# Pooled and masked attention feeding a gated layer: one form for every pair of heads, masks loaded apart, weight bits shifted in SBUF, pooled values on two engines, and a new written order

## The chip, the cores and the metric

The kernel runs on one core of a Trainium2 chip. The metric is the time of one execution on the device in microseconds (us), as the median of several runs. A profile is one further execution, recorded by the hardware profiler; its span is the time from the first to the last instruction.

## The reference

```python
def attention(q, k, v):              # 8 batches, 8 heads, 576 positions, 64 numbers per head
    q_d, k_d, v_d = means of four neighbouring positions           # 144 positions
    out_d = softmax(q_d @ k_d.T / 8) @ v_d
    scores = where(abs(i - j) < 4, q @ k.T / 8, -1e9)              # a band of seven keys
    return repeat(out_d, 4) + softmax(scores) @ v

def gated(x):                        # x: 8 x 576 x 512, the heads side by side
    h = gelu(x @ w_in)               # w_in 512 x 1024
    u, v = halves of h
    v = (v - mean(v)) / sqrt(var(v) + 1e-6) * g_ln
    v = w_sg @ v + b_sg              # w_sg 576 x 576, over positions
    return x + (u * v) @ w_out       # w_out 512 x 512
```

`w_in` and `w_out` reach the kernel as 64-bit floats, seen as pairs of 32-bit words; all else is fp32.

## The kernel before, in words

**Attention.** The eight heads of a batch go in pairs: four pairs per batch, 32 pairs in all, numbered g = 0 to 31. The local part takes a pair in ten tiles of 58 queries by 64 keys. Each pair runs through short tasks, named by letters and the pair's number:

- `lq`, `lk`, `lv`, `lw` load q, k and two layouts of v. `qs` and `ks` sum q and k over four positions (line 391 on VectorE, lines 394 and 395 on Pool). `vs` pools v in four additions (lines 408 and 409, Pool).
- `S` are the local scores (line 424), `Y` the pooled scores (line 445), both on TensorE; `YS` is one task with both.
- `ma` and `mb` add the mask to the scores and move them from PSUM to SBUF (line 432, VectorE). `mx` and `my` take the maxima (lines 454 to 456, 466 and 468, VectorE), `nx` and `ny` turn them into biases, `ea`, `eb` and `ec` are the exponentials (lines 484 and 492, ScalarE), `re` and `rc` the sum and its reciprocal (lines 497 to 503), `np` and `nq` divide.
- `T`, `U`, `t` transpose the probabilities on TensorE (lines 512 and 521); `pa`, `pb`, `pc`, `pe` copy them out (line 221). `D` multiplies them by the values (line 573 the pooled part, line 589 the local part, TensorE). `oe`, `od`, `xa`, `xb` put both parts together into x (lines 554 to 596), and `xh`, `xl`, `xc` split x into a high and a low part for products of three terms (lines 221 and 608).

**Early forms.** `EARLY_S` and `EARLY_D` are 4: pairs 0 to 3 differ from the others. Their mask is put into PSUM by TensorE, as a product of an identity matrix with the mask (line 417), and the scores are added on top of it. Their maxima (`mx`) are read from PSUM, and so are their exponentials. Their v is not pooled: line 573 runs once for each of the four positions of a group, so `D` has four times as many pooled products, with `v4` in place of `vd`; and `lv` loads v in four transfers, not two.

**Weights.** Twelve blocks of the 64-bit weights (`y0` to `y3`, `z0` to `z3`, `r0` to `r3`) are turned into fp32: `w` loads, `wq` scales the high word (line 305 on VectorE, line 303 on ScalarE), `wu` treats the low word, `wb` shifts the bits in two VectorE operations (line 309 writes a PSUM buffer, line 311 reads it and the word and writes SBUF), `wt` adds both (Pool, line 319), `wh` and `wl` split the result into a high and a low part.

**The gated layer** of batch b follows its four pairs: `v` (line 691, the products in batch 0 in four pieces `vk`), its gelu, its statistics (lines 721 to 760; line 740 normalises on VectorE), `u`, `s` and `o` (line 769) with their own tasks, and the stores `os`. Its first product, v of batch b, needs the low part of x of the batch's last pair, so `xl3` for batch 0 and `xl7` for batch 1.

**What sets the order.** `ORDER` is a string that names every task once, with an engine where a task has a choice (`/V` VectorE, `/P` Pool, `/A` ScalarE, `/S` SP). Tasks are issued in its order; each engine works through its own in that order. `place` walks the same string and gives each task its buffers out of 8 of PSUM (`ps`), 10 (`X`) and 38 (`R`) of SBUF. `T` is TensorE. SP issues nearly all loads. One constant, `small`, holds the masks, the identity, two turning matrices and g, and is one transfer.

## Time and profile before

| | before |
|---|---|
| median of 3 runs | 589.13 us |
| runs, from and to | 587.82 to 589.57 us |
| span of the profiled execution | 585.7 us |
| TensorE busy | 559.7 us (96% of the span) |
| VectorE busy | 432.7 us (74%) |
| ScalarE busy | 354.0 us (60%) |
| Pool busy | 306.2 us (52%) |

The span leaves out what lies around the program: it is 3.4 us below the median of the runs. In rows of the profile PE is TensorE, PEld its loading of weights, DVE is VectorE, ACT ScalarE, POOL GpSimd (here Pool) and SP the engine that issues loads. L573 is line 573. A group of instructions reads: line, engine, operation, output and input by the program's names, tile, shape, type, count, then busy time, mean ns of one, and the engine's idle time just before them with what ended it. A row of waits reads: engine, tile and line that waited, what released it, and the total, the number and the longest of these waits.

### The profile page before, as it was taken

The page shows a single profiled execution, that of the slowest core. Times are in us where ns is not written, and L with a number is a line of the kernel's source. Part 1 is how long each engine was busy: PE and PEld are TensorE (multiplying, and loading weights), DVE is VectorE, ACT ScalarE, POOL GpSimd, SP SyncE. Part 2 cuts the span into 40 slices and gives each one's busy share as a digit, 9 for nine tenths or more (in the row PEclk, how much of TensorE's full clock was granted, in tenths as well). Part 3 has the DMA queues.
Part 4 walks back from the last instruction along what each step waited for, and adds up shares of the span by engine and source line. Part 5 has one row for each costly group of instructions (what it writes and reads, how often), then busy time and mean ns, then how long its engine had stood idle before and what let it go on. Part 6 is the DMA issues. An engine that isn't in the chain of part 4 may idle for free.

```text
span 585.7 us, 17441 instructions
## 1 busy us (share of the span) xinstructions
PE 559.7 (96%) x6992; PEld 522.2 (89%) x6992; DVE 432.7 (74%) x947; ACT 354.0 (60%) x1227; POOL 306.2 (52%) x384
## 2 busy tenths in 40 slices
PE   4778999999999999999999999999999999999997
...
DVE  3957998968795998886658786777668877652662
...
PEclk9879999999999999999999999999999999999999
DMA  8999014534503321242046052241117430300103
GB/s 318 305 281 286 14 48 128 158 118 137 144 26 98 97 83 58 96 157 63 16 134 193 13 194 90 59 134 42 37 62 230 118 100 1 113 1 1 41 2 121
DMA packets 30610, 63.21 MB, mean 108 GB/s; under 512 B 3520, under 2 KB 3776, under 8 KB 30528
## 3 DMA queue, kind: packets, MB, share of 16 engines
...
q10 hardware_dynamic: 576, 1.23, 0.6%
q14 instruction: 27, 0.22, 0.1%
...
## 4 chain that ended last, share of the span: by engine, by line
PE 81%; DVE 8%; ACT 5%; issue 3%; DMA 1%; POOL 0%; SPq 0%; ACTq 0%; DVEq 0%; POOLq 0%
PE ps L769 49%; PE ps L691 15%; PE ps L573 4%; ACT X L484 3%; PE ps L512 3%; PE ps L589 3%; PE ps L424 2%; PE ps L445 2%; PE ps L521 2%; DMA small_sb<-in_small_dram 1%; ACT pd L492 1%; DVE R L740 1%; DVE wsg_l L352 1%; DVE st L721 1%; ACT L492 1%
## 5 line engine op out<-in xcount | busy, mean ns | idle before, releaser
L769 PE MATMUL ps<-wsg_h,R 128*128 128x288 f32 x576 | 120.8, 297 | 0.0
L769 PE MATMUL ps<-R,weight_r 128*128 128x288 f32 x768 | 109.4, 297 | 0.3 <-ACT pd L492 0.3
L769 PE MATMUL ps<-X,weight_z 128*128 128x288 f32 x512 | 108.2, 296 | 0.3 <-DVE X L432 0.3
L769 PEld LDWEIGHTS ps<-R,weight_r 128*128 128x128 f32 x768 | 103.8, 188 | 2.1 <-DVE R L826 0.4
L691 PE MATMUL ps<-weight_y,X 128*128 128x512 f32 x320 | 98.0, 400 | 0.1
L484 ACT ACTIVATE X<-X,nb 128x64 f32<-128x64 f32 x280 | 93.5, 338 | 3.2 <-DVE nb L463 2.8
L769 PEld LDWEIGHTS ps<-wsg_h,R 128*128 128x128 f32 x576 | 94.2, 188 | 0.2
L769 PE MATMUL ps<-wsg_l,R 128*128 128x288 f32 x320 | 92.8, 296 | 0.4 <-DVE wsg_l L352 0.4
L769 PEld LDWEIGHTS ps<-X,weight_z 128*128 128x128 f32 x512 | 83.9, 188 | 1.2 <-ACT weight_z L221 0.7
L769 PE MATMUL ps<-R,weight_z 128*128 128x288 f32 x256 | 75.4, 295 | 0.0
L691 PEld LDWEIGHTS ps<-weight_y,X 128*128 128x128 f32 x320 | 58.2, 189 | 12.5 <-POOL X L221 0.4
L769 PEld LDWEIGHTS ps<-wsg_l,R 128*128 128x128 f32 x320 | 60.2, 188 | 0.6 <-DVE wsg_l L352 0.6
L732 POOL TENSOR_TENSOR rs<-rs,nhalf 128x1 f32<-128x1 f32 (+1 forms) x40 | 24.5, 614 | 63.0 <-DVE rs L723 62.9
L807 DVE SCALAR_TENSOR_TENSOR vs<-ps,small_sb,b_sb 128x288 f32<-128x288 f32 x64 | 32.4, 513 | 32.6 <-PE ps L769 31.6
L484 ACT ACTIVATION_READ_ACCUMULATOR X<-X,nb 128x1 f32 x280 | 53.1, 190 | 0.0
L691 PE MATMUL ps<-weight_y,R 128*128 128x512 f32 x128 | 50.7, 396 | 0.0
L408 POOL TENSOR_TENSOR pairs<-R 112x256 f32<-112x256 f32 x56 | 44.6, 796 | 10.2 <-DMA R<-in_v_dram 10.2
L788 ACT ACTIVATE R<-ps 128x288 f32<-128x288 f32 x64 | 24.7, 411 | 40.9 <-PE ps L769 40.8
L221 ACT CAST R<-R 128x512 fp32r<-128x512 f32 (+2 forms) x44 | 28.0, 641 | 34.0 <-DVE R L814 14.2
L769 PEld LDWEIGHTS ps<-R,weight_z 128*128 128x128 f32 x256 | 48.1, 188 | 0.3
L826 POOL TENSOR_TENSOR R<-R,R 128x576 fp32r<-128x576 f32 x21 | 31.1, 1484 | 28.6 <-PE ps L521 14.4
L814 POOL TENSOR_TENSOR R<-R,vs 128x288 f32<-128x288 f32 x23 | 20.4, 894 | 45.2 <-DVE vs L807 39.2
...
## 6 DMA issues: line engine op xcount, KB each, us to landing
...
```

What stands on the lines that cost most here:

```text
L221: (nc.scalar.copy if e == "A" else ENG[e].tensor_copy)(**kw)
L408: ENG[e].tensor_tensor(out=pairs, in0=v[:, 0:2], in1=v[:, 2:4], op=ALU.add)
L484: nc.scalar.activation(out=st["ms"][:, t, :], in_=src, func=AF.Exp, bias=st["nb"][:, t:t + 1], scale=scale, accum_out=sums[par][:, t:t + 1])
L512: nc.tensor.matmul(out=out, lhsT=st["ms"][0:LD, 2 * c:2 * c + 2, :], rhs=turn_l, is_transpose=True, start=True, stop=True)
L573: nc.tensor.matmul(out=out, lhsT=lhsT, rhs=pdt[ks, probs, h * QC:(h + 1) * QC], start=first, stop=last)
L691: nc.tensor.matmul(out=acc, lhsT=r32(l), rhs=r32(weights[f"y{k}"][:, 0, w]), start=(i == 0 and ks[0] == 0), stop=(i == len(ops) - 1 and ks ...
L732: nc.gpsimd.tensor_tensor(out=rs[0:n], in0=rs[0:n], in1=nhalf[0:n], op=ALU.pow)
L769: nc.tensor.matmul(out=acc[:, 0:HALF], lhsT=r32(l), rhs=r32(r), start=(first and n == 0), stop=(last and n == len(ops) - 1))
L788: nc.scalar.activation(out=us[i // 2][:, half(i)], in_=at["ps", "m", b, "u", i][:, 0:HALF], func=AF.Gelu_apprx_tanh)
L807: nc.vector.scalar_tensor_tensor(out=vsb[i], in0=at["ps", "m", b, "s", i][:, 0:HALF], scalar=g_sb[:, i // 2:i // 2 + 1], in1=b_sb[:, half( ...
L814: ENG[e].tensor_tensor(out=u[:, half(i)], in0=u[:, half(i)], in1=vsb[i], op=ALU.mult)
L826: ENG[e].tensor_tensor(out=r32(gl[d]), in0=us[d], in1=gh[d], op=ALU.subtract)
```

## The change

- `EARLY_S`, `EARLY_D` and all that depends on them are gone. Every pair runs `YS`, adds its mask on VectorE (`ma`, `mb`), takes maxima and exponentials from SBUF, and pools its v.
- `small` is split: the masks are a constant of their own, `mask`, in its own transfer; the identity is gone; `small` keeps the turning matrices and g. Both may be loaded from SP or ScalarE.
- The shift of the weight bits (`wb`) writes the SBUF buffer of the result and works in it; the PSUM buffer is gone.
- `vs` may run on VectorE or Pool. The new string gives pairs 0, 1, 2, 5 and 6 to VectorE, 3, 4 and 7 to Pool; of all 32 pairs, 16 go to each.
- The loads of the first four pairs may be issued by ScalarE's queue; before, those of the first two.
- The string `ORDER` is new throughout.

```diff
-wy0 lk0/A lq0/A lq1/A small ks0/P wqy0/A wuy0 wby0 wty0 wy3 qs0/V S0 mx0 lw1/A qs1/P nx0/V ea0 why0/V wqy3/V Y0 my0
...
-EARLY_S, EARLY_D = 4, 4
...
-    small_sb = const.tile([P, 7 * KB + P + LD + 2 * QD + KT], F32, name="small_sb")
...
+    mask_sb = const.tile([P, 7, KB], F32, name="mask_sb")
+    small_sb = const.tile([P, LD + 2 * QD + KT], F32, name="small_sb")
...
-    add("small", {"S": 0.5}, lambda e: nc.sync.dma_start(out=small_sb, in_=small), mb=0.4)
+    add("mask", {"S": 0.5, "A": 0.5}, lambda e: DQ[e].dma_start(out=mask_sb.rearrange("p t k -> p (t k)"), in_=masks), mb=0.22)
+    add("small", {"S": 0.5, "A": 0.5}, lambda e: DQ[e].dma_start(out=small_sb, in_=small), mb=0.17)
...
-        keys = ("R", "w", t), ("ps", "b", t)
+        key = "R", "w", t
...
         def shift(e):
-            bits, done, hw = like(buf(*keys[1])).bitcast(I32), like(buf(*keys[0])).bitcast(I32), word(1)
-            nc.vector.tensor_scalar(out=bits, in0=hw.bitcast(I32), scalar1=3,
+            done, hw = like(buf(*key)).bitcast(I32), word(1)
+            nc.vector.tensor_scalar(out=done, in0=hw.bitcast(I32), scalar1=3,
                                     scalar2=0x7FFFFFF8, op0=ALU.logical_shift_left, op1=ALU.bitwise_and)
-            nc.vector.scalar_tensor_tensor(out=done, in0=hw.bitcast(I32), scalar=-0x80000000, in1=bits,
+            nc.vector.scalar_tensor_tensor(out=done, in0=hw.bitcast(I32), scalar=-0x80000000, in1=done,
                                            op0=ALU.bitwise_and, op1=ALU.bitwise_or)
...
-                for rows in (slice(0, QC), slice(HD, QD)) if early_d else (slice(0, QD),):
-                    DQ[e].dma_start(out=st["v4"][i][rows], in_=v4[b, p, i, rows].rearrange("j (f d) -> j f d", f=FAC))
+                DQ[e].dma_start(out=st["v4"][i], in_=v4[b, p, i].rearrange("j (f d) -> j f d", f=FAC))
...
-            if early:
-                for i in range(2):
-                    nc.tensor.matmul(out=sp[i][:, 0:NW[i] * KB], lhsT=ident_sb, rhs=mask_sb[:, MB[i]:MB[i] + NW[i], :],
-                                     start=True, stop=False, skip_group_check=True)
-            for t in (0, 4, 1, 5, 2, 6, 3, 7, 8, 9) if early else (4, 5, 0, 6, 1, 7, 2, 8, 3, 9):
+            for t in (4, 5, 0, 6, 1, 7, 2, 8, 3, 9):
...
-            if early:
-                for i in range(2):
-                    nc.vector.tensor_reduce(out=stats[par][:, i * NA:i * NA + NW[i]], in_=spv(i), axis=AX.X, op=ALU.max)
-            else:
-                nc.vector.tensor_reduce(out=stats[par][:, 0:NT], in_=st["ms"], axis=AX.X, op=ALU.max)
+            nc.vector.tensor_reduce(out=stats[par][:, 0:NT], in_=st["ms"], axis=AX.X, op=ALU.max)
...
-                    src = spv(i)[:, c] if early else st["ms"][:, t, :]
-                    nc.scalar.activation(out=st["ms"][:, t, :], in_=src, func=AF.Exp, bias=st["nb"][:, t:t + 1],
+                    nc.scalar.activation(out=st["ms"][:, t, :], in_=st["ms"][:, t, :], func=AF.Exp, bias=st["nb"][:, t:t + 1],
...
-                lhsT = st["v4"][t][ks, f, hs] if early_d else st["vd"][ks, t, hs]
...
-            for f in fs:
-                for i in range(2):
-                    for h in range(2):
-                        pooled(i, h, f, 0, slice(0, 3), slice(0, 3))
+            for i in range(2):
+                for h in range(2):
+                    pooled(i, h, 0, slice(0, 3), slice(0, 3))
...
-        if not early_d:
-            add(N("vs"), {"P": 2.7}, vsum, [N("lv"), N("D", 2)], gives=[("R", "v4", g, 0), ("R", "v4", g, 1)])
+        add(N("vs"), {"P": 2.7, "V": 1.1}, vsum, [N("lv"), N("D", 2)], gives=[("R", "v4", g, 0), ("R", "v4", g, 1)])
```

The start of VectorE's queue, before: `nb0` and `stats0` belong to pair 0's local softmax, `weight_y0` is the first weight block, `qd0` holds the row sums of q.

```order
L309 TENSOR_SCALAR ps0_127<-weight_y0_113 128x512
L311 SCALAR_TENSOR_TENSOR R3_128<-weight_y0_113,ps0_127 128x512
L391 TENSOR_REDUCE qd0_75<-R1_117 128x144
L454 TENSOR_REDUCE stats0_79<-ps1_135 128x4
L454 TENSOR_REDUCE stats0_79<-ps2_136 128x6
L463 TENSOR_SCALAR nb0_90<-stats0_79 128x10
```

And after; the lines of the changed code stand a few above those of before (L387 sums, L423 adds the mask, L443 and L453 to L455 take maxima, L305 to L311 are the weights).

```order
L387 TENSOR_REDUCE qd0_76<-R0_114 128x144
L387 TENSOR_REDUCE qd1_77<-R2_119 128x144
L453 TENSOR_REDUCE stats0_80<-ps2_128 128x2
L455 TENSOR_REDUCE stats0_80<-ps3_129 128x1
L462 TENSOR_SCALAR nbd0_93<-stats0_80 128x3
L423 TENSOR_TENSOR X0_206<-ps0_138,mask_sb_70 128x256
L423 TENSOR_TENSOR X0_206<-ps1_139,mask_sb_70 128x384
L443 TENSOR_REDUCE stats0_80<-X0_206 128x10
L305 TENSOR_SCALAR weight_y2_210<-weight_y2_210 128x512
```

The row sums of two pairs and the whole first softmax now stand ahead of the first weight block, and the masks are added here.

The first product D (pair 0) in TensorE's queue, before: R15 and R16 hold the unpooled values, R17 the transposed pooled probabilities. Each of these rows stands four times in a turn; two of the first kind, and one of each other, are shown.

```order
L573 MATMUL ps7_413<-R17_386,R15_377 64x144 x2
L573 MATMUL ps5_414<-R17_386,R15_377 64x144 x2
L573 MATMUL ps7_413<-R17_386,R15_377 64x144 x2
L573 MATMUL ps5_414<-R17_386,R15_377 64x144 x2
...
L573 MATMUL ps7_413<-R17_386,R16_378 64x48 x2
L573 MATMUL ps5_414<-R17_386,R16_378 64x96 x2
...
L589 MATMUL ps7_413<-R14_364,X3_383 64x58 x2
```

And after, where L555 is the pooled part, L570 the local one, and vd0 holds the pooled values of pair 0.

```order
L555 MATMUL ps1_467<-R17_423,vd0_86 64x144 x2
L555 MATMUL ps3_468<-R17_423,vd0_86 64x144 x2
L555 MATMUL ps1_467<-R17_423,vd0_86 64x48 x2
L555 MATMUL ps3_468<-R17_423,vd0_86 64x96 x2
L570 MATMUL ps1_467<-R10_357,X4_464 64x58 x2
```

32 pooled products have become 8, and `vd0` has to be there first.

Between the third products of batch 0 and batch 1's first in TensorE's queue, after (L742 are the products `u`, `s` and `o`, here `s` with wsg_h and wsg_l; L436 and L416 are scores, L664 is v): the first row ends `s` of one half, and the last begins batch 1.

```order
L742 MATMUL ps7_1753<-wsg_l_74,R30_1290 128x288
L555 MATMUL ps3_1778<-R36_1773,vd1_87 64x144 x2
...
L570 MATMUL ps1_1779<-R16_1740,X9_1424 64x58 x2
L742 MATMUL ps5_1808<-wsg_h_73,R28_1129 128x288
...
L742 MATMUL ps5_1808<-wsg_l_74,R30_1290 128x288
L436 MATMUL ps4_1845<-kd0_84,qd0_76 64x144 x2
...
L416 MATMUL ps6_1856<-R17_1513,R25_1420 64x64 x2
L664 MATMUL ps1_1889<-weight_y0_380,X1_1731 128x512 x2
```

In before the third products of batch 0 end at a row of wsg_l as well, and what follows them is this, up to a product `o` of batch 0 and then batch 1.

```order
L769 MATMUL ps5_1581<-wsg_l_73,R18_1376 128x288
L512 MATMUL ps4_1597<-small_sb_70,X8_1191 128x122 x4
L573 MATMUL ps6_1602<-R13_1470,vd1_86 64x144 x2
...
L445 MATMUL ps7_1632<-kd1_84,qd1_76 64x144 x2
...
L769 MATMUL ps0_1946<-R1_1698,weight_r2_1540 128x288
...
L691 MATMUL ps7_2081<-weight_y0_172,X5_1378 128x512 x2
```

Most of batch 0's `o` products stand ahead of batch 1's v before, and all of them behind it after.

More of the change, by code (lines that the diff above doesn't have):

```diff
@@ L189 @@
[L189 to L192 removed]
+lq0/S lk0/A qs0/V lq1/A qs1/V lk1/S mask/S ks0/P YS0 my0 ny0/V ks1/P YS1 ec0 lq2/S qs2/P ma0 mb0 mx0 wy2 wqy2/V wuy2
@@ new lines @@
+ny9/V lw11 s0.5 mx8 xh6/A xl6/P pc7/A pe7/A qs11/V mb9 D7 s0.6 ec9 wqr2/A oe7/A od7 xa7 xb7 nx8/A ea8 gh0.1/A xh7/V
+sa0.5 gh0.0/A wur1 YS10 ma10 whr3/A eb8 xl7/V v1.0 v1.2 sm0.5/V sa0.7 re8/A ks11/P wbr0 u1.4 mx9 nx9/V ea9 wbr2 v1.1
+my10 ny10/V wbr1 wtr1 xc6 lk12 rc8 mb10 eb9 ks12/V ua1.4 vg1.2 vg1.0 nq8/V wtr0 np8/P sm0.4/P xc4 vg1.1 wur2 whr1/A
+u1.6 T8 ua1.6 mx10 xc7 sm0.7/P vb1.0 U8 vb1.1 u1.7 t8 nx10/A ea10 sa0.6 u1.5 vs8/P re9/V pa8/V pb8/V pc8/A pe8/A vs9/V
+wlr3/V ec10 xc5 eb10 gl0.0/P rc9 nq9/P ua1.5 v1.4 va1.4/V wtr2 whr2/A YS11 my11 gh0.2/V ny11/A vb1.2 ma11 vj1.4
@@ L212 @@
     w_out: bass.AP,
+    masks: bass.AP,
     small: bass.AP,
@@ L330, in weight64 @@
         add(f"wq{t}", {"A": 0.56, "V": 0.7}, scaled, [f"w{t}"])
-        add(f"wb{t}", {"V": 1.42}, shift, [f"wq{t}"], takes=keys, gives=keys[1:])
+        add(f"wb{t}", {"V": 1.42}, shift, [f"wq{t}"], takes=[key])
         add(f"wt{t}", {"P": 1.3}, total, [f"wb{t}", f"wu{t}"])
         add(f"wh{t}", {"A": 0.56, "V": 0.4}, high, [f"wt{t}"])
-        add(f"wl{t}", {"P": 1.3, "V": 0.66}, low, [f"wh{t}"], gives=keys[:1])
+        add(f"wl{t}", {"P": 1.3, "V": 0.66}, low, [f"wh{t}"], gives=[key])
     for k in range(KT):
@@ L363, in attention @@
         g = b * NPAIR + p
-        N = lambda c, back=0: f"{c}{g - back}" if g >= back and not (c == "vs" and g - back < EARLY_D) else None
+        N = lambda c, back=0: f"{c}{g - back}" if g >= back else None
         par = g % 2
-        SN = lambda back=0: N("S" if g - back < EARLY_S else "YS", back)
-        YN = lambda back=0: N("Y" if g - back < EARLY_S else "YS", back)
-        early, early_d = g < EARLY_S, g < EARLY_D
         def load_q(e):
@@ L424, in scores @@
                     nc.tensor.matmul(out=sp[i][os, c * KB:(c + 1) * KB], lhsT=q[hs, t * QB:t * QB + KB],
-                                     rhs=k[hs, t * QB:t * QB + KB], start=not early, stop=True,
-                                     skip_group_check=early)
+                                     rhs=k[hs, t * QB:t * QB + KB], start=True, stop=True)
         def masked(i):
@@ L638, in attention @@
-        add(N("mx"), {"V": 0.95 if early else 0.8}, top, ([SN()] if early else [N("ma"), N("mb")]) + [N("nx", 2)])
+        dq = {"S": 0.5, "A": 0.5} if g < 4 else {"S": 0.5}
+        add(N("lq"), dq, load_q, [N("YS", ahead), N("qs", ahead)], takes=[("R", "q", g)], mb=0.3)
+        add(N("lk"), dq, load_k, [N("YS", ahead), N("ks", ahead)], takes=[("R", "k", g)], mb=0.3)
+        add(N("lv"), dq, load_v4, [N("D", ahead // 2)], takes=[("R", "v4", g, 0), ("R", "v4", g, 1)], mb=0.3)
+        add(N("lw"), dq, load_vw, [N("D", ahead)], takes=[("X", "vw", g)], mb=0.33)
```

281 lines of the change are left out of this document (131 added, 150 removed).

## The prediction, made before the changed kernel ran

> **What bounds the kernel now.** I read the page's first two parts, then the windows, then the waits of the first 60 us, then the order of both programs. The page first: its row of engines, and TensorE, VectorE, clock and DMA in 40 slices of 14.6 us each.
>
> ```profile
> PE 559.7 (96%) x6992; PEld 522.2 (89%) x6992; DVE 432.7 (74%) x947; ACT 354.0 (60%) x1227; POOL 306.2 (52%) x384
> ...
> PE   4778999999999999999999999999999999999997
> ...
> DVE  3957998968795998886658786777668877652662
> ...
> PEclk9879999999999999999999999999999999999999
> DMA  8999014534503321242046052241117430300103
> ```
>
> TensorE is full from slice 5 on and not before; the loads fill slices 1 to 4. The windows: each stretch and its length, the busy time (and instructions) of TensorE, its weight loads, VectorE, ScalarE and Pool, the granted clock, the DMA share and GB/s:
>
> ```profile
> 60.00:100.00 40.00, 39.31 (x363) 36.52 (x363) 37.57 (x71) 36.95 (x101) 29.48 (x32) 1.00 0.20 60
> 5.00:100.00 95.00, 81.02 (x1192) 70.17 (x1193) 76.38 (x159) 74.89 (x277) 67.71 (x74) 0.93 0.63 202
> 100.00:200.00 100.00, 98.67 (x1437) 91.70 (x1436) 81.51 (x186) 75.00 (x281) 62.00 (x80) 1.00 0.37 113
> 0.00:100.00 100.00, 81.02 (x1192) 70.17 (x1193) 76.77 (x162) 76.17 (x278) 68.87 (x82) 0.93 0.63 200
> ...
> 60.00:500.00 440.00, 436.20 (x5494) 409.98 (x5494) 349.39 (x771) 302.40 (x1023) 237.54 (x301) 1.00 0.31 95
> ```
>
> Of 26.0 us in which TensorE does nothing (585.7 less 559.7), 19.0 lie in the first 100 us, and only 3.8 between 60 and 500 us. So two things count: how much TensorE has to do, and when it can go on without a gap. From 60 to 100 us VectorE is busy for 37.57 of 40 us and TensorE for 39.31: both are at their end there. Who waits for what before 60 us, TensorE first, then VectorE:
>
> ```profile
> PE ps L417 <- DMA small_sb<-in_small_dram: 8.5, 1, 8.5
> PE ps L573 <- issue: 5.2, 2, 3.1
> ```
>
> ```profile
> DVE ps L309 <- ACT weight_y L303: 5.5, 1, 5.5
> DVE da L556 <- PE ps L589: 5.1, 3, 2.7
> DVE R L221 <- PE ps L521: 4.3, 2, 4.1
> DVE stats L454 <- PE ps L424: 2.5, 1, 2.5
> ```
>
> VectorE stands still for 17.4 us in these four rows, 11.9 of them for TensorE, whose early products (L417, L573) are the ones that the change takes away.
>
> **The change, part by part.** *TensorE loses work.* The forms that go and the one that stays, whole run:
>
> ```profile
> L573 PE MATMUL ps<-R,vd 48*64 48x144 f32 x224 | 13.7, 305 | 0.0
> ...
> L573 PE MATMUL ps<-R,vd 48*64 48x96 f32 x112 | 9.3, 243 | 0.0
> L573 PE MATMUL ps<-R,vd 48*64 48x48 f32 x112 | 7.6, 211 | 0.0
> L573 PE MATMUL ps<-R,R 48*64 48x144 f32 x128 | 7.1, 340 | 2.4 <-issue 2.0 <-DVE X L432 0.3
> L573 PE MATMUL ps<-R,R 48*64 48x96 f32 x64 | 4.5, 289 | 0.0
> L417 PE MATMUL ps<-small_sb 128*128 128x384 f32 x8 | 4.1, 602 | 0.3 <-DVE R L311 0.3
> L573 PE MATMUL ps<-R,R 48*64 48x48 f32 x64 | 3.4, 248 | 3.1 <-issue 3.1
> L417 PE MATMUL ps<-small_sb 128*128 128x256 f32 x8 | 3.3, 502 | 8.5 <-DMA small_sb<-in_small_dram 8.5
> ```
>
> Mask products 4.1 + 3.3, unpooled values 7.1 + 4.5 + 3.4: 22.4 us go. The pooled form costs (13.7 + 9.3 + 7.6) / 28 = 1.09 us per pair, 4.4 us for four pairs. Net 18.0 us less. If every idle gap stayed, the span would be 567.7 us.
>
> *The gaps will not stay.* All 18 us lie before 60 us, where TensorE waits anyway. What counts is when batch 1's first product (v1.0) can begin; behind it TensorE has work without a gap in either order. In the old order, batch 0's third products (s0) end at 101.61 us. The new order has more ahead of v1.0: scores of four more pairs (YS7 to YS10), D of pairs 5 to 7, and the turns T, U, t of pairs 6 and 7. Their lengths, at full clock, from the timeline of before, where one stands behind the other: T from 101.61, D from 102.12, YS from 103.11, U from 104.29 to 104.67, t from 106.34 to 106.46:
>
> ```profile
> 101.61 0.58 PE L512 MATMUL ps<-small_sb,X 122*128 122x122 f32 x4
> 102.12 0.63 PE L573 MATMUL ps<-R,vd 48*64 48x144 f32 x15
> ...
> 103.11 0.29 PE L445 MATMUL ps<-kd,qd 64*64 64x144 f32 x1
> ...
> 104.29 0.32 PE L512 MATMUL ps<-small_sb,X 122*128 122x122 f32 x1
> ...
> 104.67 1.83 PE L769 MATMUL ps<-R,weight_r 128*128 128x288 f32 x12
> 106.34 0.35 PE L521 MATMUL ps<-small_sb,pd 112*112 112x112 f32 x2
> 106.46 1.84 PE L769 MATMUL ps<-R,weight_r 128*128 128x288 f32 x12
> ```
>
> T is 0.51, D 0.99, YS 1.18, U 0.38, t 0.12. Four YS, three D and two of each turn are 4.72 + 2.97 + 2.02 = 9.7 us; at the 98.67% of the 100 to 200 us window, 9.8. So before has done the same work at 111.4 us, and 474.3 us follow.
>
> *VectorE sets the new place.* v1.0 needs the low half of x of pair 7 (xl7, on VectorE). By the order, 209 VectorE instructions stand from the first row sum to xl7. Before's VectorE took 76.77 us for 162 in its first 100 us (474 ns each) and 81.51 for 186 in the next (438 ns). Taken together, 455 ns: 95.1 us of work, bounds 91.6 and 99.1. That count holds what the change adds on VectorE: masks added and a maximum of SBUF in place of two maxima of PSUM in four pairs, and four pooling additions in each of pairs 0, 1, 2, 5 and 6. When can it start? The first transfer of k and its row sum on Pool, before:
>
> ```profile
> 6.19 0.67 POOL L394 TENSOR_TENSOR half<-R 128x288 f32<-128x288 f32 x1 [4.50 <-DMA R<-in_kT_dram]
> 6.93 0.43 POOL L395 TENSOR_TENSOR kd<-half 128x144 f32<-128x144 f32 x1
> ```
>
> q of pair 0 should land about then too, as the first on SP. VectorE makes two row sums, then waits for YS0, which cannot start before kd is there (7.4) and takes 1.18: about 1 us is lost. Counted as one late start: between 5.4 (less load ahead of it) and 7.1 us; I take 6.6. How dense is VectorE behind it? 37.57 / 40 = 0.94 where it is the one at its end (60 to 100 us), 76.38 / 95 = 0.80 over 5 to 100 us, with the 11.9 us of waits for TensorE in it. TensorE is no longer short of time in the new order: it has 81.0 - 18.0 + 9.8 = 73 us to do by v1.0. So I take 0.94: 95.1 / 0.94 = 101.2, v1.0 at 107.8 us instead of 111.4. Span 107.8 + 474.3 = 582.1; with the 3.4 us between the profiled span (585.7) and the median (589.13), **585.5 us, 0.6% faster**. Of 18 us taken away, 14 go into waiting.
>
> *The shift of the weight bits.* Nine of its twelve stand ahead of v1.0. What runs there, and the nearest forms with both sides in SBUF:
>
> ```profile
> L740 DVE TENSOR_SCALAR R<-R,mv,rs 128x512 f32<-128x512 f32 x32 | 20.8, 654 | 2.8 <-POOL rs L732 2.7
> ...
> L309 DVE TENSOR_SCALAR ps<-weight_z 128x512 int32<-128x512 int32 x4 | 2.8, 689 | 0.3 <-ACT pd L492 0.3
> ...
> L305 DVE TENSOR_SCALAR weight_z<-weight_z 128x512 f32<-128x512 f32 x1 | 0.4, 361 | 0.0
> ```
>
> From 689 ns the first operation goes to 361 at best (L305), and by L740's mean, of the same shape in a busy stretch, to 654. I take the second, 0.3 us in all; the first would give 3.0. Both stay in the range. The Trainium skill (VectorE: DVE Perf Modes, "The perf-mode tier table") says that a one-input fp32 operation on VectorE runs at twice the rate when both sides are in SBUF, and not with PSUM on one side. By that alone the place would come 3.0 us earlier; L305's row agrees with it, L740's mean of the same shape does not.
>
> *Company on SBUF.* The same operation on 13 columns, VectorE, twice:
>
> ```profile
> 39.62 0.16 DVE L499 TENSOR_SCALAR sums<-sums 128x13 f32<-128x13 f32 x1
> ...
> 93.50 0.85 DVE L499 TENSOR_SCALAR sums<-sums 128x13 f32<-128x13 f32 x1
> ```
>
> The second is 0.69 us longer. The change puts 20 pooling additions and nine two-input shifts of SBUF on VectorE ahead of v1.0, while Pool runs. If a quarter of the 29 lose 0.69 us each it is 5.0 us, which would end the gain; the mean of 455 ns holds such losses at before's rate, so I add nothing and keep 5 us for the upper end. The Trainium skill (GPSIMD Engine Reference, "Specifications") says that Pool shares its SBUF interfaces with VectorE and contends with VectorE instructions of two SBUF inputs or in a two-port mode; that rule speaks against this change, and the 0.85 us row bears it out.
>
> *Transfers, ScalarE, tail.* By the sizes of the loads that stand ahead of v1.0 in the new order, about 23 MB come in by then; the values of the first four pairs come in two transfers each, not four, so SP issues eight fewer. Pool pools v of three of the first eight pairs, where it did four. At before's pace, 17.60 MB in 62 us (row below), that is 81 us: hidden by 27 us of VectorE's time. ScalarE's exponentials of four pairs read SBUF in place of PSUM; it has the same work as before otherwise and is hidden by VectorE; if it were not, it would cost its own delay one to one. In the last batch nothing of the change applies; I leave before's idle time there, with 2 us to either side for the new order.
>
> ```profile
> DMA packets 8330, 17.60 MB, mean 284 GB/s; under 512 B 960, under 2 KB 960, under 8 KB 8320
> ```
>
> **The rivals.** *A, the whole 18 us come through* (571.1 us): TensorE's gaps stay as they are. For it: 5.2 us of TensorE's early waits sit inside the very products that go, and they leave more room. Against: 209 VectorE instructions would have to be done by 93 us, at a density of 1.10. Only cheaper instructions would allow it. Chance 0.12.
>
> *B, VectorE falls behind and the kernel gets slower.* The place is VectorE's queue in the first 100 us. It works in order, and between its own steps it waits for exponentials of ScalarE, products at a low clock (PEclk begins 9, 8, 7, 9) and Pool. The point from which it decides: 95.1 / (111.4 - 6.6) = 0.907 of density. Below that the new order loses. At before's own 0.80 it is v1.0 at 125.5, span 599.8, 603.2 us; at 0.87, 593.7. For it: 0.80 is what VectorE reached in before. Against: 11.9 us of its waits were for TensorE; with them taken out of the 95 us it is 76.38 / 83.1 = 0.92. Chance 0.26.
>
> *C, the loads set the pace as they do now* (589 us, no change): if SP's queue, where a load that waits for a free buffer holds back those behind it, loses the 27 us. For it: the DMA row is full in slices 1 to 4. Against: it is not in slices 5 and 6. Chance 0.12.
>
> **How the numbers follow.** The forecast has 0.50. About 0.3% (1.8 us) is what a measurement can tell from no change. Of the forecast's 0.50, 0.42 is faster by more than that and 0.08 within; A adds 0.12 faster; B 0.21 slower and 0.05 within; C 0.10 within and 0.02 slower. Faster 0.54, within 0.23, slower 0.23. The range reaches from 576 (v1.0 at 98: the 91.6 us of work, and the shifts at their best) to 597 (a density of 0.84), and leaves out about half of A and the slow end of B.
>
> **What would show it.** Right: TensorE's busy time is near 542 us and its idle time near 40; v1.0's first product (weight_y, 128x512, after a row of wsg products) starts near 108 us; VectorE is at 0.94 from 10 to 105 us; the waits for L417 and "issue" at L573 are gone. Wrong: v1.0 before 102 us or after 113; VectorE waiting for ScalarE or DMA for over 10 us in the first 100; the shift's first operation at 0.4 us throughout; more than 12 us of idle TensorE time behind v1.0.

## The result and the profile after

The changed kernel takes 608.81 us (median of 4 runs, 607.55 to 609.30) beside 588.48 us for the kernel before (now the median of 4 runs): ratio 1.0351, interval 1.0319 to 1.0383. It is 3.5% slower; forecast were 585.5 us and a range of 576 to 597. The lines of the changed code are new: L742 are the products u, s and o, L664 is v, L436 and L416 are scores, L555 and L570 are D, L423 adds the mask, L462 is the pooled bias, L404 and L405 pool v, L589 is the low half of x.

The page after: engines, and TensorE, VectorE, clock and DMA in 40 slices of 15.2 us.

```profile
span 607.5 us, 17056 instructions
...
PE 565.5 (93%) x6784; PEld 522.6 (86%) x6784; DVE 466.4 (77%) x999; ACT 348.5 (57%) x1218; POOL 307.4 (51%) x367
...
PE   3679989699999999999999999999999998999997
...
DVE  5999999989988775895688789686747757683652
...
PEclk9659999899999999999999999999999998999999
DMA  8997356001282223320142414530045222000302
```

VectorE is at 9 in each of slices 2 to 8, where before had 9, 5, 7, 9, 9, 8 and 9; TensorE has a hole in slice 8. Batch 1's first product, which was forecast at 107.8 us, comes at 119.4. The windows ahead of it and behind it (columns as before):

```profile
20.00:120.00 100.00, 81.58 (x1181) 69.51 (x1180) 96.12 (x181) 72.49 (x278) 74.39 (x78) 0.86 0.64 188
0.00:119.40 119.40, 90.34 (x1408) 77.48 (x1408) 109.20 (x211) 82.77 (x328) 86.23 (x101) 0.86 0.69 209
119.40:607.50 488.10, 475.17 (x5378) 445.11 (x5376) 357.25 (x789) 265.77 (x891) 221.22 (x266) 0.99 0.25 79
```

VectorE is as dense as was assumed (96.12 of 100 us; 0.94 in the forecast), and the number of its instructions is right (211; 209 counted from the first row sum). But each takes 109.20 / 211 = 518 ns of busy time, not 455. Behind the place 488.1 us follow, 13.8 more than the 474.3 of the forecast. The two misses, 11.6 and 13.8 us, are the whole error of the span (607.5 less 582.1).

What VectorE waits for up to 130 us, and TensorE's largest waits there:

```profile
DVE qd L387 <- DMA R<-in_qT_dram: 5.1, 2, 4.1
DVE X L423 <- PE ps L416: 1.3, 2, 0.7
```

```profile
PE ps L436 <- POOL kd L391: 8.0, 2, 6.7
PE ps L496 <- POOL X L490: 4.0, 1, 4.0
PE ps L555 <- DVE vd L405: 3.7, 5, 1.5
PE ps L436 <- ACT pd L476: 3.3, 1, 3.3
```

The waits of VectorE that the prediction quoted (17.4 us) are gone, TensorE's for L417 and for "issue" at L573 as well. Behind its first loads VectorE hardly waits any more; its instructions got longer. The groups of the added work up to 119.4 us, and the row sums (L387) for comparison:

```profile
L404 DVE TENSOR_TENSOR pairs<-R 112x256 f32<-112x256 f32 x10 | 8.6, 856 | 0.0
...
L462 DVE TENSOR_SCALAR nbd<-stats 128x3 f32<-128x3 f32 x4 | 6.9, 1731 | 0.0
...
L405 DVE TENSOR_TENSOR vd<-pairs 112x128 f32<-112x128 f32 x10 | 5.7, 574 | 0.3
...
L311 DVE SCALAR_TENSOR_TENSOR R<-weight_z,R 128x512 int32<-128x512 int32 x4 | 4.5, 1117 | 0.1
L311 DVE SCALAR_TENSOR_TENSOR R<-weight_y,R 128x512 int32<-128x512 int32 x4 | 3.9, 980 | 0.1
...
L309 DVE TENSOR_SCALAR R<-weight_y 128x512 int32<-128x512 int32 x4 | 3.1, 764 | 0.0
...
L387 DVE TENSOR_REDUCE qd<-R 128x144 f32<-128x576 f32 x4 | 3.0, 745 | 5.1 <-DMA R<-in_qT_dram 5.1
```

L404 takes 362 ns at its fastest and 856 on average; the two-input half of the shift 691 and 1117. A bias of three numbers takes 1731 on average, because one took 6.40 us. It stands beside Pool like this; VectorE first, then Pool:

```profile
107.43 0.46 DVE L787 TENSOR_TENSOR R<-R,vs 128x288 f32<-128x288 f32 x1
107.81 6.40 DVE L462 TENSOR_SCALAR nbd<-stats 128x3 f32<-128x3 f32 x1
114.13 0.80 DVE L443 TENSOR_REDUCE stats<-X 128x10 f32<-128x640 f32 x1
```

```profile
107.65 0.56 POOL L405 TENSOR_TENSOR vd<-pairs 112x128 f32<-112x128 f32 x1
108.17 2.79 POOL L589 TENSOR_TENSOR R<-R,X 128x576 fp32r<-128x576 f32 x2
110.92 1.29 POOL L319 TENSOR_TENSOR R<-R,weight_r 128x512 int32<-128x512 int32 x1
112.17 1.40 POOL L589 TENSOR_TENSOR R<-R,X 128x576 fp32r<-128x576 f32 x1
113.52 0.66 POOL L390 TENSOR_TENSOR half<-R 128x288 f32<-128x288 f32 x1
114.27 0.42 POOL L391 TENSOR_TENSOR kd<-half 128x144 f32<-128x144 f32 x1
```

Pool's five instructions from 108.17 to 114.19 start without a pause; the first pause is at 114.19 to 114.27, ahead of L391, which needs the result of the instruction in front of it. There the bias ends. ScalarE's exponentials wait for it, and TensorE's scores for them:

```profile
114.31 0.38 ACT L476 ACTIVATE pd<-ps,nbd 128x144 f32<-128x144 f32 x1 [6.30 <-DVE nbd L462]
```

```profile
115.56 0.46 PE L436 MATMUL ps<-kd,qd 64*64 64x144 f32 x4 [3.27 <-ACT pd L476]
```

Take each of VectorE's instructions up to the place, and its duration less the shortest of its own line, names and shape in the run. The sum is 31.3 us, against 8.7 in before up to 111 us. Without it the 211 instructions would average (122.2 - 31.3) / 211 = 431 ns and before's 184 would average (96.8 - 8.7) / 184 = 479 ns (their durations overlap a little at the ends), so the new mix is not longer by itself. 27.6 of the 31.3 us lie on arithmetic instructions from SBUF to SBUF with one or two inputs; no instruction with PSUM on a side and no reduction took over 0.08 us more than its shortest.

The 6.40 us are the exception among these delays. 23 instructions ahead of the place took 0.4 us or more over their shortest; for 21 of them the delay ends with the one Pool instruction that ran when they began (0.08 to 0.17 us ahead of its end). In 12 of the 23 the next Pool instruction follows without a pause, as here (VectorE, then Pool):

```profile
102.11 1.63 DVE L311 SCALAR_TENSOR_TENSOR R<-weight_r,R 128x512 int32<-128x512 int32 x1
```

```profile
101.93 1.26 POOL L490 TENSOR_TENSOR X<-X,rc 128x640 f32<-128x640 f32 x1 [2.52 <-ACT nbd L460]
103.14 1.36 POOL L493 TENSOR_TENSOR pd<-pd,rc 128x432 f32<-128x432 f32 x1
```

At its shortest this L311 takes 0.69 us, so it got in at about 103.0, and it is the Pool instruction behind it that took 0.45 us over its shortest. In before, 6 instructions up to 111 us were so late.

**Theory 1:** VectorE's instructions with two SBUF inputs, and its short one-input ones from SBUF to SBUF, stand behind Pool's; the change put many of them beside a busy Pool. Some of the expectations below say it more strictly, that they start only when Pool pauses; the 12 above contradict that. **Theory 2:** VectorE has too much to do by then, whatever Pool does. **Theory R and F,** on the part behind: the new order of the rest is slower by itself (R), or the late front carries on (F).

### The profile page after: what moved, and what is told of

Read it like the earlier page. It is cut to its first block, busy times and chain, and to the rows that moved or that the text cites. A ratio compares the mean times of both kernels' runs of the same rounds, so it can differ in the third digit from the quotient of the medians.

```text
span 607.5 us, 17056 instructions
## 1 busy us (share of the span) xinstructions
PE 565.5 (93%) x6784; PEld 522.6 (86%) x6784; DVE 466.4 (77%) x999; ACT 348.5 (57%) x1218; POOL 307.4 (51%) x367
## 3 DMA queue, kind: packets, MB, share of 16 engines
q1 hardware_dynamic: 30384, 61.69, 32.7%
## 4 chain that ended last, share of the span: by engine, by line
PE 39%; DVE 5%; ACT 4%; POOL 1%; issue 1%; DMA 0%; ACTq 0%; POOLq 0%
PE ps L742 27%; PE ps L664 6%; ACT X L468 2%; PE ps L570 1%; PE ps L496 1%; PE ps L555 1%; POOL R L733 1%; PE ps L436 1%; PE ps L505 1%; DVE vd L405 1%; PE ps L416 1%; ACT R L222 1%; DMA R<-in_kT_dram 0%; ACT L761 0%; DVE R L816 0%
## 5 line engine op out<-in xcount | busy, mean ns | idle before, releaser
L742 PE MATMUL ps<-wsg_h,R 128*128 128x288 f32 x576 | 123.8, 301 | 3.2 <-DVE R L577 1.5
L742 PE MATMUL ps<-X,weight_z 128*128 128x288 f32 x512 | 112.7, 301 | 3.8 <-DVE X L423 2.4
L468 ACT ACTIVATE X<-X,nb 128x64 f32<-128x64 f32 x320 | 107.0, 340 | 10.2 <-DVE nb L450 9.8
L742 PE MATMUL ps<-R,weight_r 128*128 128x288 f32 x768 | 108.8, 297 | 0.7 <-DVE R L799 0.7
L742 PEld LDWEIGHTS ps<-R,weight_r 128*128 128x128 f32 x768 | 103.4, 188 | 2.3 <-DVE R L799 1.1
L664 PE MATMUL ps<-weight_y,X 128*128 128x512 f32 x320 | 98.9, 404 | 1.2 <-DVE R L577 0.5
L742 PEld LDWEIGHTS ps<-wsg_h,R 128*128 128x128 f32 x576 | 93.9, 188 | 5.2 <-DVE R L577 1.7
L742 PE MATMUL ps<-wsg_l,R 128*128 128x288 f32 x320 | 92.7, 295 | 0.4 <-POOL wsg_l L352 0.4
L742 PEld LDWEIGHTS ps<-X,weight_z 128*128 128x128 f32 x512 | 85.6, 190 | 5.6 <-DVE X L423 2.7
L742 PE MATMUL ps<-R,weight_z 128*128 128x288 f32 x256 | 76.0, 297 | 0.0
L664 PEld LDWEIGHTS ps<-weight_y,X 128*128 128x128 f32 x320 | 58.9, 191 | 14.0 <-DVE weight_y L326 0.9
L468 ACT ACTIVATION_READ_ACCUMULATOR X<-X,nb 128x1 f32 x320 | 61.4, 192 | 0.0
L742 PEld LDWEIGHTS ps<-wsg_l,R 128*128 128x128 f32 x320 | 60.3, 188 | 0.6 <-POOL wsg_l L352 0.6
L222 ACT CAST R<-R 128x512 fp32r<-128x512 f32 (+2 forms) x44 | 27.5, 639 | 53.1 <-POOL R L787 27.6
L664 PE MATMUL ps<-weight_y,R 128*128 128x512 f32 x128 | 51.4, 401 | 0.4 <-DVE R L589 0.4
L742 PEld LDWEIGHTS ps<-R,weight_z 128*128 128x128 f32 x256 | 48.7, 190 | 0.6
L490 POOL TENSOR_TENSOR X<-X,rc 128x640 f32<-128x640 f32 x25 | 33.8, 1351 | 27.6 <-DVE rc L487 17.4
L222 ACT COPY R<-ps 112x192 f32<-112x192 f32 (+3 forms) x71 | 26.1, 391 | 32.1 <-PE ps L505 15.5
L436 PE MATMUL ps<-kd,qd 64*64 64x144 f32 (+2 forms) x512 | 28.9, 294 | 16.7 <-POOL kd L391 8.0
```

The costliest lines, as they stand in the source:

```text
L222: (nc.scalar.copy if e == "A" else ENG[e].tensor_copy)(**kw)
L436: nc.tensor.matmul(out=st["sdv"][n][os, cs], lhsT=qd2[par][hs, i * QC:i * QC + HD], rhs=st["kd"][hs, ks], start=True, stop=True)
L468: nc.scalar.activation(out=st["ms"][:, t, :], in_=st["ms"][:, t, :], func=AF.Exp, bias=st["nb"][:, t:t + 1], scale=scale, accum_out=sums[p ...
L490: ENG[e].tensor_tensor(out=st["ms"], in0=st["ms"], in1=bc_last(st["rc"][:, 0:NT], KB), op=ALU.mult)
L664: nc.tensor.matmul(out=acc, lhsT=r32(l), rhs=r32(weights[f"y{k}"][:, 0, w]), start=(i == 0 and ks[0] == 0), stop=(i == len(ops) - 1 and ks ...
L742: nc.tensor.matmul(out=acc[:, 0:HALF], lhsT=r32(l), rhs=r32(r), start=(first and n == 0), stop=(last and n == len(ops) - 1))
```

## The experiments

Ratios are to the kernel before on the same chip. "Place" is the start of batch 1's first product in the one profiled execution of each kernel.

**Instructions that should not stand behind Pool.** e1 pools v with reductions, e2 moves biases, e12 does both.

```diff
 e1      for i, v in enumerate(st["v4"]):
+            if e == "V":
+                nc.vector.tensor_reduce(out=vd[:, i], in_=v.rearrange("p f d -> p d f"), axis=AX.X, op=ALU.add)
+                continue
 e2  ORDER: sixteen times
-ny9/V
+ny9/A
```

> The changed kernel, in its own order, with v pooled on VectorE by one reduction per half (512 elements read, 128 written) in place of two additions of two SBUF inputs each. Theory 1 (VectorE's short one-input and its two-input instructions on SBUF wait for Pool's instruction to end): the 64 additions took 37.7 us in the changed kernel's trace, the 32 reductions take 0.65 to 0.75 us each, 21 to 24 us, as the row sums of 576 elements at 0.745 us were never slowed; VectorE loses about 15 us, 7 of them ahead of batch 1's first product, which moves from 119.4 to 112 to 114 us; 595 to 601 us. Theory 2 (VectorE simply has more instructions than it can do by then, long ones and short ones alike): 64 additions at their fastest, 0.36 and 0.29 us, are the same work as the reductions; 608 us, no change.

> The changed kernel with the 16 pooled biases that VectorE does (3 numbers a row, one of which took 6.40 us at 107.81 us) moved to ScalarE. Theory 1: that one was a wait for five Pool instructions in a row; without it VectorE reaches batch 1 about 5 us sooner and TensorE's wait of 3.3 us before the scores at 115.6 us goes; 602 to 605 us. Theory 2: sixteen instructions of 0.16 us are 2.6 us of VectorE's work in the whole run; 607 to 609 us, no change.

> The changed kernel with v pooled on VectorE by reductions and the pooled biases on ScalarE, both of which do not stand behind Pool. Alone they brought batch 1's first product from 119.4 to 115.2 and to 112.8 us. Theory 1 (the front's loss is VectorE behind Pool): the gains add up, it comes at 108 to 110 us, as forecast for an undisturbed VectorE; time 597 to 602, ratio 1.018 to 1.027, the rest of the loss staying behind it. Rival (something else ends the front by about 113 us): 112 to 114 us, ratio 1.029 to 1.034.

e1: ratio 1.0318 (1.0272 to 1.0363), place 115.2. e2: 1.0339 (1.0289 to 1.0389), place 112.8. e12: 1.0253 (1.0209 to 1.0298), place 110.1. The first row is e1's reduction up to 120 us; the others are the place in e2 and in e12.

```profile
L404 DVE TENSOR_REDUCE vd<-R 112x128 f32<-112x512 f32 x10 | 10.1, 1052 | 0.0
```

```profile
112.80 0.73 PE L664 MATMUL ps<-weight_y,X 128*128 128x512 f32 x2
```

```profile
110.14 0.73 PE L667 MATMUL ps<-weight_y,X 128*128 128x512 f32 x2
```

The reduction is never slowed (1017 to 1077 ns in e12's front, 1009 to 1098 in its whole run), but costs 1.05 us, not 0.7, so e1 gained 4.2 us of place where 5 to 7 were expected. Its time, 604.0 us, is above the 595 to 601 expected as well, and its bias of three numbers still takes 6.43 us. The gains of e1 and e2 nearly add (4.2 + 6.6 = 10.8 by the sum, 9.3 measured). By theory 2 neither would have moved the place. The times of e1 and e2 alone decide nothing, since their intervals overlap the changed kernel's; their places do, and e12's time. The times follow by less than the place: e2's span is 603.4, 4.1 less for 6.6 us of place.

**What Pool does, changed.** e17 moves one task of Pool; e18 takes its long run away.

```diff
 e17 ORDER
-vs7/P xh5/A xl5/P xh4/A xl4/P
+vs7/P xh5/A xl5/P ks11/P xh4/A xl4/P
...
-re8/A ks11/P wbr0
+re8/A wbr0
 e18 ORDER: xl4, xl5 and xl6
-xl4/P
+xl4/V
```

> The changed kernel with one task moved in its order: the sums of k of pair 11 (two Pool instructions, the second of which needs the first) go from behind the low halves of x of pairs 5, 4 and 6 to just behind the first of them; all engines keep their work. In the changed kernel Pool ran five instructions with no pause from 108.17 to 114.19 us, and VectorE's pooled bias of 3 numbers took from 107.81 to 114.21. Theory 1 (VectorE gets in only when Pool pauses): the pause between the two sums now comes at about 110.2 us, the bias ends there, after 2.4 us; batch 1's first product 2.5 to 4 us sooner, at 115.5 to 117. Rival (Pool's mere activity slows that instruction, or the wait is for something else): still 5 to 6.4 us, at 119 us. The time follows by half at most, 604 to 608 us.

> The changed kernel with the low halves of x of pairs 4, 5 and 6 on VectorE, in their places. Theory 1: Pool's run without a pause is gone, no VectorE instruction of the front takes over 2.5 us, though VectorE has three instructions of 0.75 us more; batch 1's first product at 115 to 118 us. Rival (VectorE's amount of work sets the place): it comes later, at 120 to 122 us.

e17: ratio 1.0271 (1.0233 to 1.0310), place 114.1, better than the 115.5 to 117 expected, and 0.8% of the time for one moved task. The bias, and Pool beside it:

```profile
107.30 2.42 DVE L462 TENSOR_SCALAR nbd<-stats 128x3 f32<-128x3 f32 x1
```

```profile
107.66 1.41 POOL L589 TENSOR_TENSOR R<-R,X 128x576 fp32r<-128x576 f32 x1
109.04 0.66 POOL L390 TENSOR_TENSOR half<-R 128x288 f32<-128x288 f32 x1
109.77 0.43 POOL L391 TENSOR_TENSOR kd<-half 128x144 f32<-128x144 f32 x1
110.16 1.43 POOL L589 TENSOR_TENSOR R<-R,X 128x576 fp32r<-128x576 f32 x1
```

2.42 us, as foretold from Pool's pause (109.70 to 109.77). e18: 1.0318 (1.0284 to 1.0352), which overlaps the changed kernel's interval; place 116.3, 3.1 us sooner with more work on VectorE, where theory 2 said later. One sign was missed: a VectorE instruction of 2.88 us (L589 at 107.81) where none over 2.5 was expected. e17 shows that a pause of Pool ended the long wait of the bias; e18 speaks against the amount of VectorE's work.

**The shift.** e3 puts it into SBUF in the kernel before; e14 puts ten of twelve back through PSUM, in e12's kernel.

```diff
 e3
-bits, done, hw = like(buf(*keys[1])).bitcast(I32), like(buf(*keys[0])).bitcast(I32), word(1)
+buf(*keys[1])
+done, hw = like(buf(*keys[0])).bitcast(I32), word(1)
+bits = done
 e14
+bits = like(buf("ps", "b", t)).bitcast(I32) if t in IN_PSUM else done
```

> The kernel before with one part of the change: the shift of the weight bits works in SBUF, order and all else as before (the PSUM buffer is still reserved). Theory 1: its 24 instructions, 0.69 us each before whatever Pool did, spread from 0.36 to 1.6 us by what Pool is doing; the one-input half gets shorter where Pool is idle, the two-input half longer; 16.7 us become 16 to 24; time 588 to 592 us. Theory 2 (both sides in SBUF is only the faster form): 13 us, 585 to 588 us.

> The same last run's kernel with ten of its twelve shifts (all but z0 and r1) through a PSUM buffer again, where one is free in its order. Theory 1 (operations with PSUM on a side don't stand behind Pool): all 20 of these instructions take 0.68 to 0.70 us; those ahead of batch 1's first product took about 5 us over their fastest time, 3 to 4 of it in the two-input half; it comes 2 to 3 us sooner, at 107 to 108 us; ratio 1.020 to 1.025. Rival (a bank taken for the shift holds back scores or turns): 110 to 112 us, ratio 1.025 to 1.032.

e3: 1.0044 (1.0012 to 1.0075). The 24 instructions take 22.9 us in place of before's 16.5, and the place is 126.6, 3.0 us later. Three groups of e3, and two of before:

```profile
L313 DVE SCALAR_TENSOR_TENSOR R<-weight_z,R 128x512 int32<-128x512 int32 x4 | 5.6, 1403 | 0.1
L313 DVE SCALAR_TENSOR_TENSOR R<-weight_r,R 128x512 int32<-128x512 int32 x4 | 3.9, 977 | 0.1
...
L311 DVE TENSOR_SCALAR R<-weight_y 128x512 int32<-128x512 int32 x4 | 3.2, 806 | 5.4 <-ACT weight_y L303 5.4
```

```profile
L311 DVE SCALAR_TENSOR_TENSOR R<-weight_r,ps 128x512 int32<-128x512 int32 x4 | 2.7, 687 | 0.1
...
L309 DVE TENSOR_SCALAR ps<-weight_r 128x512 int32<-128x512 int32 x4 | 2.7, 685 | 0.0
```

With PSUM on one side the 24 lie between 676 and 695 ns; in SBUF between 416 and 1686. e14: 1.0277 (1.0256 to 1.0298), place 113.6 against 110.1 in e12: a miss; the time, but not the place, lies in the range of its rival. The shifts do take 0.68 us again, but now another instruction meets Pool's run of five (102.27 to 108.36):

```profile
102.34 6.34 DVE L793 TENSOR_TENSOR R<-R,vs 128x288 f32<-128x288 f32 x1
```

**Pooled v.** e4 moves 14 pairs to VectorE in the kernel before; e5 moves all 16 back to Pool in the changed one; e6 adds e2's change to e5.

```diff
 e4 ORDER: vs 5, 6, 9, 10, 11, 13, 14, 17, 19, 21, 23, 24, 29, 31
-vs5
+vs5/V
 e5 ORDER
-vs5/V
+vs5/P
```

> The kernel before with another part alone: v of 14 pairs (5, 6, 9, 10, 11, 13, 14, 17, 19, 21, 23, 24, 29, 31) pooled on VectorE in place of Pool, order as before. Theory 1: the 56 additions take 0.5 to 0.6 us each on average, not 0.33, with single ones over 1 us; VectorE's busy time rises from 433 to 455 to 465 us; TensorE is full there, so the time rises by little, 588 to 594 us. Theory 2: 56 additions at 0.33 us, VectorE at 450 us, the time unchanged.

> The changed kernel with v of all 32 pairs pooled on Pool (16 pairs moved back from VectorE), its order otherwise kept. In the old order the same move the other way, for 14 pairs, made the time 2.3% longer. Theory 1 (pooled v on VectorE is dear, because each addition stands behind Pool's): VectorE loses 38 us of 466 and batch 1's first product comes at about 108 us, as forecast; 592 to 599 us, ratio to before 1.01 to 1.02. Theory 2 (the new order loses the time by itself, in the places that it gives to the tasks): Pool gets 16 times 2.5 us and is as late as VectorE was; 604 to 612 us.

> The changed kernel with all pooled v on Pool and the pooled biases on ScalarE. Theory 1: both gains add up ahead of batch 1's first product (it came 6.6 us sooner with the biases alone); 588 to 595 us. Theory 2: 600 to 608 us.

e4: 1.0234 (1.0187 to 1.0282), more than expected. Its additions on VectorE, with Pool freed of 33 us, still average 515 and 388 ns:

```profile
L408 DVE TENSOR_TENSOR pairs<-R 112x256 f32<-112x256 f32 x28 | 14.4, 515 | 0.0
...
L409 DVE TENSOR_TENSOR vd<-pairs 112x128 f32<-112x128 f32 x28 | 10.9, 388 | 1.0
```

e5: 1.0417 (1.0392 to 1.0442), e6: 1.0455 (1.0435 to 1.0475), places 120.7 and 119.0. Here theory 1's forecast fell. VectorE had 12 us less to do ahead of the place, but the new order gives Pool its tasks as if it had no v to pool, and TensorE then waits longer for Pool than in the changed kernel (8.0, 4.0 and 3.7 us in the rows shown above, the last of them for VectorE there). e5, up to 121 us:

```profile
PE ps L436 <- POOL kd L391: 11.8, 3, 6.7
PE ps L496 <- POOL X L490: 5.7, 2, 3.9
PE ps L555 <- POOL vd L405: 3.7, 4, 1.5
```

So pooling on VectorE is dear in the old order and the lesser evil in the new one; a task's engine cannot be priced apart from the order.

**Early forms, and all forms at once, in the old order.** e7 drops the unpooled products, e8 both early forms (both pool v of pairs 0 to 3 on Pool, with `vs0` to `vs3` put into the order); e11 is e8 with e3's shift and v of 17 pairs on VectorE.

```diff
 e7
-EARLY_S, EARLY_D = 4, 4
+EARLY_S, EARLY_D = 4, 0
 e8
-EARLY_S, EARLY_D = 4, 4
+EARLY_S, EARLY_D = 0, 0
 ORDER
-S0 mx0 lw1/A
+YS0 ma0 mb0 mx0 lw1/A
```

> The kernel before with one part of the change: v of pairs 0 to 3 pooled (on Pool, just ahead of pe) in place of unpooled products; order otherwise kept. TensorE loses 15.0 us of unpooled products and gets 3.3 of pooled ones. Theory 1 (TensorE is not what sets the early places; VectorE and Pool are): no gain; Pool's 10 us more come early, 585 to 592 us. Rival (TensorE's long early products are what VectorE waits for): 575 to 581 us.

> The kernel before with both early forms gone, v of pairs 0 to 3 on Pool, masks of pairs 0 to 3 added on VectorE, order otherwise kept, with YS 0 and 1 where S 0 and 1 stood and YS 2 and 3 where Y 2 and 3 stood. TensorE loses 18 us; VectorE gets about 3 us more. Theory 1: no gain, 586 to 594 us. Rival: 570 to 579 us.

> All of the change's forms in the old order: no early forms (YS 0 to 3 as in the run without early forms), v of pairs 0 to 2, 5, 6, 9 to 11, 13, 14, 17, 19, 21, 23, 24, 29 and 31 pooled on VectorE, the shift in SBUF. Alone, they cost 1.15% (no early forms, v on Pool), 2.34% (v on VectorE) and 0.44% (shift). If the forms are what costs and the order gives little: 1.034 to 1.046. If each form takes the same slack: 1.023 to 1.030.

e7: 1.0019 (1.0002 to 1.0037). e8: 1.0115 (1.0094 to 1.0137). e11: 1.0372 (1.0327 to 1.0417); the parts alone add to 1.15 + 2.34 + 0.44 = 3.9%. TensorE in e8 and two of its waits up to 60 us:

```profile
PE 551.5 (93%) x6784; PEld 517.0 (87%) x6784; DVE 433.7 (73%) x951; ACT 355.2 (60%) x1227; POOL 316.8 (54%) x400
```

```profile
PE ps L513 <- POOL X L507: 11.9, 3, 8.7
PE ps L446 <- DVE qd L392: 9.4, 1, 9.4
```

TensorE loses 559.7 - 551.5 = 8.2 us, not 18.0, and the idle time before batch 1's first product rises from 19.5 to 32.7 us: the removed products became waiting, and then some. With all forms in the old order the time is that of the changed kernel within the intervals, but it is lost in other places: e11 has batch 1's first product at 131.5 us, 12.1 later than the changed kernel, and takes 411.9 us from batch 2's first product on, 5.6 less.

**The part behind.** e9 joins the new order up to the place to the old one behind it; e10 is the reverse; e13 joins them at batch 2's first product, with e12's forms; e15 is e13 with e14's shift.

The change is in the string: for e9, e13 and e15 the new one up to that product and then, in the old order, the tasks that are left; for e10 the other way round. Pooled v of the rest is on Pool in e9, e13 and e15, and partly on VectorE in e10.

> The changed kernel with its new order up to batch 1's first product, and from there the old order of all tasks that are left (pooled v of the rest on Pool, as there). In the changed kernel that product came at 119.4 us, and 488.1 us followed, 13.8 more than the 474.3 worked out from before. Theory R (those 13.8 us come from the new order of the rest, with its pooled v on VectorE): 119 and 474 to 478, span 593 to 597, ratio to before 1.013 to 1.020. Theory F (a late front carries its backlog on, whatever order follows): 1.030 to 1.038.

> The other half: the kernel before, early forms and old shift and old order up to batch 1's first product, and from there the new order of all that is left, with its choice of engines (pooled v of the rest on VectorE or Pool). The product should come at 123.6 us as before. Theory R: 13 to 14 us are lost behind it; span 598 to 601, ratio 1.020 to 1.027. Theory F: 0.998 to 1.006.

> The kernel of the last run (changed kernel, reductions, pooled biases on ScalarE) in its new order up to batch 2's first product, and the old order for all that is left from there, pooled v of the rest on Pool. At that place both orders have done the same products but one (U12 more in the new), so that there is hardly a seam. It came at 180.4 us in that run and at 180.5 in before; from there to the end it took 417.4 us in the new order and 405.2 in the old. Theory R (the order of the rest, with pooled v between VectorE and Pool, loses 12 us by itself): 180 and 405 to 408, span 585 to 588, ratio to before 0.998 to 1.007. Theory F (what came before batch 2 leaves VectorE behind): 1.015 to 1.026.

> Both: reductions, pooled biases on ScalarE, ten shifts through PSUM, new order up to batch 2's first product and the old one behind it. If theories 1 and R hold and their gains add: batch 2's first product at 178 us, 406 behind it, span 582 to 585, ratio 0.993 to 1.001: the 18 us of products that were taken out give at most 0.5%. If not: above 1.010.

e9: 1.0419 (1.0370 to 1.0468). e10: 1.0586 (1.0541 to 1.0631). e13: 1.0114 (1.0081 to 1.0147). e15: 1.0121 (1.0088 to 1.0154), with a wait of 6.34 us like e14's at 101.02; its gains did not add. The times of e9 and e10 lie outside the ranges of both theories: they lost at the seam; in e9 the weights of o come late:

```profile
PE ps L742 <- POOL weight_r L326: 7.0, 1, 7.0
PE ps L742 <- ACT weight_r L222: 6.2, 1, 6.2
```

So their totals decide nothing, but what follows batch 2's first product does. Starts of the batches' first products in us, from the timelines:

| | batch 1 | batch 2 | batch 3 | end of span | batch 2 to end |
|---|---|---|---|---|---|
| before | 123.6 | 180.5 | 251.8 | 585.7 | 405.2 |
| e9, old rest | 146.6 | 203.2 | 275.9 | 610.3 | 407.1 |
| e13, old rest | 110.3 | 180.5 | 255.7 | 590.2 | 409.7 |
| changed | 119.4 | 190.0 | 261.5 | 607.5 | 417.5 |
| e10, new rest | 131.2 | 202.1 | 273.5 | 617.5 | 415.4 |
| e12, new rest | 110.1 | 180.4 | 251.9 | 597.8 | 417.4 |
| e4, old rest, v on VectorE | 123.6 | 184.8 | 256.0 | 595.8 | 411.0 |

The rest takes what its own order takes (405 to 412 in all kernels with the old one, 415 to 419 in all with the new), whatever the front did: R, not F. e13's miss (1.0114 for at most 1.007) is one step, batch 2 to 3, 75.2 us in place of 71.3; from batch 3 on it takes 334.5, before 333.9. The table also shows that e12's front reaches batch 2 just when before does.

**The remedy in the old order.** e16 moves the 25 biases that VectorE does in the kernel before to ScalarE.

```diff
 ORDER: nx and ny
-nx8/V
+nx8/A
```

> The kernel before with the 25 biases that VectorE does (3 and 10 numbers a row) on ScalarE, to see whether what helped the new order's front helps the old one. Ahead of batch 1's first product two of them stood 0.9 us over their fastest time in all. Theory 1: at most 1 us; 0.997 to 1.003. Rival (ScalarE, 60% busy, becomes late): 1.004 to 1.010.

1.0100 (1.0065 to 1.0135): theory 1's forecast was wrong for it, and the time lies at the upper end of the rival's range; the place came 1.2 us sooner (122.4), and 5.3 us were lost behind. That ScalarE became late, as the rival has it, was not shown. None of the eighteen kernels beats the one before.

## Why the prediction was wrong, step by step

- **VectorE sets the new place: right, but by another link.** Its start (5.3 us; forecast 6.6), its density (0.95 from there to the place; 0.94) and its count hold. The low half of x of pair 7 is not what the first product waits for: it is made from 119.67 to 120.42, while that product runs from 119.41. It stands behind scores in TensorE's queue, and those waited, by way of ScalarE, for VectorE's 6.40 us bias. Rival B named that place too, but for a wrong reason: VectorE was not thinned out by waits.
- **"Taken together, 455 ns": the first of the two steps that failed.** It took before's mean for a new mix beside a busy Pool. 518 - 455 = 63 ns by 209 is 13 us, more than the 11.6 by which the place was late. The prediction saw the danger (0.69 us on a quarter of 29 instructions, 5.0 us) but let the mean "hold such losses". The 20 additions alone took 14.3 us, 7.8 over their shortest, and the one bias lost 6.2. Moving the bias (e2) brought the place 6.6 us forward, moving a pause of Pool (e17) 5.3, and reductions with the biases moved (e12) 9.3 of the 11.6. The Trainium skill (SBUF — State Buffer, "SBUF: two separate sides") says that VectorE's instructions in a two-port mode or with two SBUF inputs and Pool's exclude each other for a whole instruction, the loser being blocked; the trace agrees: the delay of 21 of the 23 late instructions ends with one Pool instruction. The bias was held up by the rest of one and by five more, and why it did not get in between them as others did is not shown.
- **The shift, 0.3 us: wrong sign and size.** Up to the place its nine one-input halves average 684 ns, hardly shorter than the 689 they were reckoned from, and its nine two-input halves, which the sum left as they were, lose 3.8 us over their shortest. e3 measures 6.4 us more VectorE time for all 24 instructions, and 0.44% of the kernel's time.
- **TensorE loses 18.0 us: mis-sized.** 8.2 in e8. The groups overlap in time, so their sum is not time: counted once, all rows of the line fill 29.3 us in before (L573) and 22.0 in e8 (L574), and L417 fills 7.0, so 14.3 us go; the other 6.1 stay open. In the changed kernel TensorE's busy time, forecast near 542, is 565.5 us, for as many products as e8's 551.5 (6784); e18 has 565.0 at a granted clock of 0.997, so the clock does not explain it, and it stays open too. "The gaps will not stay" was right, and e7 shows it alone: TensorE's front loses 6.4 us, its idle time there grows as much, the place stays at 123.6.
- **474.3 us behind: wrong by 13.8, the second step that failed.** It took the new order of the rest to be as good as the old. TensorE is idle for 12.9 us behind the place, more than the 12 that were named as a sign of being wrong, and for 6.5 in before. From batch 2's first product on it is idle 6.4 us longer than in before and busy 5.9 us longer. By e9, e10, e12 and e13 the rest's own order costs 8.3 (415.4 less 407.1) to 12.3 us (417.5 less 405.2). In the old order pooled v on VectorE alone costs 5.8 of that part (e4), but in the new order the part takes 415.2 us with all v on Pool as well (e5); so which of the new order's choices cost it was not settled, and neither were the 4 us of e13's step. e1 and e2 did little for that part: 414.6 and 419.4 from batch 2 on, beside 417.5.
- **Transfers and ScalarE hidden: right.** The DMA share is 0.64 from 20 to 120 us, and VectorE waits 5.1 us for loads, all before 7.1 us, and 0.2 us for ScalarE.
